# A convolution and two expert layers in one kernel: the last group of one product is put behind the next middle stage, and seven input steps run ahead

## The chip, the cores and the metric

One NeuronCore of a Trainium2 chip runs the whole kernel as one program. The metric is device time in microseconds (us): of several runs the median counts. A profiled execution gives the trace that is read here; its times are counted from the start of its span. The engines are named as the profile names them: PE is TensorE (PEld its weight loads), DVE VectorE, ACT ScalarE, POOL GpSimd, SP SyncE; a q behind a name is the engine's own queue (SPq issues loads, ACTq and POOLq issue the DMAs of their engines).

## The reference: what is computed

```
Xf = rfft(x, n=2S); Hf = rfft(h, n=2S)      # x: 4 batches, S=5696 positions, D=128 channels
y  = irfft(Xf * Hf)[:, :S, :]               # causal convolution along the sequence
x  = moe(y.reshape(22784, 128))             # 8 experts, each takes at most 2848 tokens, in order of logit
out = moe2(x)                               # 8 experts, one per token, times its softmax weight
```

The change concerns the convolution alone. Its transform of length S = 89 * 64 is done as matrix products: a product over 89 positions (matrix F), a middle stage over 64 (matrices E, a multiplication by the transform of h, and EI), and a product back (matrix G).

## The kernel before, in words

The four batches are worked in two pairs; pair 0 is batches 0 and 1, pair 1 batches 2 and 3. `A` is one buffer in SBUF of 128 partitions x 89 x 256, and both pairs use it. Each pair passes three stages.

- **First product, `s1`** (one call per batch, 256 columns of A are two calls). 16 steps per batch: a step is 16 matmuls with F (line 99) into one PSUM tile, whose two halves are copied into A by ACT and by DVE (line 103). Four steps share one load of the input, `XB<-in_xl` (line 94). A trace counts each of these f32 matmuls twice, so a step is 32 there.
- **Middle stage, `s2`.** 23 groups of four frequencies: matmuls with E on A (line 145), multiplication by the transform of h by DVE (line 148, with `hh` loaded by line 138), sums on POOL (lines 149 and 150), matmuls with EI (line 158), a copy back into A by ACT (lines 159 and 160), and a store `Z<-A` to DRAM on ACT's queue (line 161). Between the groups of the second middle stage a search for the routing thresholds is woven in (`head.step`): DVE's small instructions, an ACT pass over VT (line 417) and two PE matmuls (line 384).
- **Last product, `s3`.** 16 groups and a closing step. A group loads `XB<-Z` in two halves (line 172; every half reads rows of all frequencies, so it needs every `Z<-A` of its pair), does 32 matmuls with G (line 179; 64 in a trace), a DVE copy of 712 columns (line 183), and, one step later, the logits of the columns that are complete (lines 195, 197, 201, 203), their transposes into rows (line 220), a copy by ACT or DVE (lines 222, 223) and a store `yrow<-m` on POOL's queue (line 225). Columns left over from a group, `carry`, are copied to the front of the next (line 182).

Six buffers XB are shared in turn by the input loads, the E loads (line 135) and the Z loads. `ps` is a pool of four PSUM tiles that all stages share; a new tile waits until the tile four before it has been copied out. `m` is a pool of three SBUF buffers, shared by line 148 and by the rows of line 225.

The order is written out by `together` (line 226): it runs `ahead` steps of the first generator, then one step of the second and `r` of the first in turn. `together(nextpair(), s3(0), 2, 4)` joins the last product of pair 0 with the first product of pair 1: four steps ahead, then two per group. Then come the second middle stage `s2(1)` and `s3(1)`. Each engine and each queue runs its instructions in the order in which they stand; a scheduler at build time moves them a little by its own costs, which is why the order of the built program is shown below.

The part behind the convolution (the routing and the two expert layers) is the same in both kernels. Its gathers and scatters of single rows (lines 777, 759, 958) are DMAs whose descriptors POOL writes into a scratch area of SBUF.

Of the kernel before, what the change touches and what calls it, by code (L numbers as in the profile page):

```python
# [11 lines left out]
F32 = mybir.dt.float32  # L12
# [41 lines left out]
def first(b):  # L54

    return -(N1*b//N2)


def conv(tc,nc,a,yrow,LG,head):

    ctx=contextlib.ExitStack()
    with ctx:
        cp=ctx.enter_context(tc.tile_pool(name="cc",bufs=1))
        Hd=ctx.enter_context(tc.tile_pool(name="cd",bufs=1,space=bass.MemoryType.DRAM)).tile([128,23,2,2,128],F32,name="Hd")
        Z=[ctx.enter_context(tc.tile_pool(name=f"cz{i}",bufs=1,space=bass.MemoryType.DRAM)).tile([96,132,256],F32,name=f"Z{i}") for i in range(2)]
# [11 lines left out]
        def pads():  # L77

            zt=work("m"); nc.gpsimd.memset(zt,0.0)
            for i in range(2):  # L80
              for k in (89,93): nc.scalar.dma_start(Z[i][k:min(k+4,96),:128].rearrange("k r e -> r k e"),zt[:,:256*(min(k+4,96)-k)].rearrange("p (k e) -> p k e",e=256))
        XB=[cp.tile([128,2048],F32,name=f'XB{i}') for i in range(6)]
        nx=[0]
        def buf():
            nx[0]+=1; return XB[nx[0]%6]
        WS=dict(xs=1224,m=1040)
        def work(nm,w=1024): return wk.tile([128,WS.get(nm,1024)],F32,name=nm)[:,:w]
        def apart(i,mine,other):
            tc.declare_no_dep(i.ins,group=other,reason='other columns of A'); tc.add_to_no_dep_group(mine,i.ins)
        def s1(src,col,free=False):  # L90

            for g in range(4):
                xt=buf()[:96].rearrange("p (d n) -> p d n",n=64); cuts=(0,8,32) if col==128 and not g else (0,32)
                for d0,d1 in zip(cuts,cuts[1:]): nc.sync.dma_start(xt[:,d0:d1],src[:,g*2048+d0*64:g*2048+d1*64].rearrange("p (d n) -> p d n",n=64))
                for q in range(4):
                    p=ps.tile([128,2,512],F32,name="ps")
                    for i in range(8):
                        for c in range(2):
                            nc.tensor.matmul(p[c*64:c*64+64,i//4,(i%4)*89:(i%4)*89+89], xt[:,q*8+i,:], F[:,c*89:c*89+89], start=True,stop=True)  # L99
                    for u in range(2):  # L100
                        c0=col+g*32+q*8+4*u
                        o=A[:,:,c0:c0+4]; i=p[:,u,:356].rearrange("p (v k) -> p k v",v=4)
                        w=nc.scalar.activation(o,i,AF.Copy) if u==0 else nc.vector.tensor_copy(o,i)
                        if free: apart(w,'x0','h')
                    yield
# [22 lines left out]
        def s2(pr,step):  # L128
# [23 lines left out]
            def back(g):  # L152
                m=ST.pop(g); k,n,nq,P=part(g)
                pb=ps.tile([128,2,2,256],F32,name="ps")
                for q in range(nq):
                    for r in range(2):
                        for t in range(min(2,n-2*q)):
                            nc.tensor.matmul(pb[:,t,q],EI[t*64:t*64+64,r],m[t*64:t*64+64,q,2*r:2*r+2],start=r==0,stop=r==1)
                if n>1: nc.scalar.activation(A[:,k:k+n,:].rearrange("p (q t) e -> p q t e",t=2),pb.rearrange("p t q e -> p q t e"),AF.Copy)
                else: nc.scalar.activation(A[:,k:k+1,:],pb[:,0,0:1],AF.Copy)  # L160
                nc.scalar.dma_start(Z[pr][k:k+n,:128].rearrange("k r e -> r k e"),A[:,k:k+n,:])
            lag=3
            for i in range(ng+lag):
                step(i)
                if i<ng: forth(i)
                if i>=lag: back(i-lag)
        def s3(pr,step):

            st=dict(carry=0,prev=None,done=0)
            def spread(g):  # L170
                Bt=buf()[:96].rearrange("p (c j e) -> p c j e",j=4,c=2)
                for c in range(2): nc.sync.dma_start(Bt[:,c],Z[pr][:,c*64+4*g:c*64+4*g+4])
                py=ps.tile([128,8,128],F32,name="ps")
                for j in range(4):
                    w=first(4*g+j)+A0
                    for b in range(2):
                        for c in range(2):
                            for t in (0,64):
                                nc.tensor.matmul(py[t:t+64,j*2+b,:89],Bt[:,c,j,b*128+t:b*128+t+64],G[:,c,w:w+89],start=c==0,stop=c==1)  # L179
                carry=st['carry']; tot=carry+712  # L180
                yT=work("xs",1224)
                if carry: nc.vector.tensor_copy(yT[:,:carry],st['prev'])
                nc.vector.tensor_copy(yT[:,carry:carry+712].rearrange("p (a b) -> p a b",b=89),py[:,:,:89])
                new=[]
                for o in range(0,tot,512):
                    n=min(4,(tot-o)//128)
                    if n==4 or g==15 and n: new.append((yT[:,o:o+n*128],n,pr*89+st['done'])); st['done']+=n
                o=sum(n for _,n,_ in new)*128
                st.update(carry=tot-o,prev=yT[:,o:tot])
                return new  # L190
            def logits(sets):

                p=ps.tile([128,2,512],F32,name="ps"); lt=wk.tile([128,384],F32,name="lt",bufs=2)
                for s,(y,n,_) in enumerate(sets):
                    for j in range(n): nc.tensor.matmul(p[32*j:32*j+32,0,s*128:s*128+128],WG,y[:,j*128:j*128+128],start=True,stop=True)
                f=sum(n==4 for _,n,_ in sets)*128
                if f: nc.vector.tensor_copy(lt[:,:f],p[:,0,:f])
                if f<len(sets)*128: nc.vector.tensor_copy(lt[:32*n,f:f+128],p[:32*n,0,f:f+128])
                return p,lt,sets
            def columns(p,lt,sets):  # L200
                for s,(_,n,_) in enumerate(sets): nc.tensor.transpose(p[:,1,s*128:s*128+32*n],lt[:32*n,s*128:s*128+128],head.Ib[:32*n,:32*n])
                n=sum(n for _,n,_ in sets); col=sets[0][2]
                nc.vector.tensor_copy(LG[:,:,col:col+n],p[:,1,:32*n].rearrange("p (c w) -> p w c",w=32)[:,:8])
                head.columns(col+n)
            new=[]
            for g in range(17):
                old=new; t=logits(old) if old else None
                if g<16: new=spread(g)
                step(g)
                if t:  # L210
                    columns(*t)
                    for u in range(0,len(old),2): rows(old[u:u+2])
                yield
            assert st['carry']==0 and st['done']==89
        def rows(sets):

            nch=sum(n for _,n,_ in sets); col=sets[0][2]
            pt=ps.tile([128,2,512],F32,name="ps"); rb=work("m",8*W1).rearrange("p (i w) -> p i w",w=W1)
            for u,(y,n,_) in enumerate(sets):
                for i in range(n): nc.tensor.transpose(pt[:,u,i*128:i*128+128],y[:,i*128:i*128+128],head.Ib)  # L220
                o=rb[:,4*u:4*u+n,:128]; i=pt[:,u,:n*128].rearrange("p (i d) -> p i d",d=128)
                if u or len(sets)==1: nc.scalar.activation(o,i,AF.Copy)
                else: nc.vector.tensor_copy(o,i)
            nc.gpsimd.tensor_copy(rb.bitcast(I32)[:,:nch,128:],idt[:,col:col+nch,:])
            nc.gpsimd.dma_start(yrow[col*128:(col+nch)*128,:].rearrange("(i p) w -> p i w",p=128),rb[:,:nch])
        def together(ga,gb,r,ahead=0):

            for _ in range(ahead): next(ga,None)
            for _ in gb:
                for _ in range(r): next(ga,None)  # L230
            for _ in ga: pass
        for i,_ in enumerate(s1(a['hl'],128)):
            if i==3: later()
        together(s2h(128),s1(a['xl'][0],0,True),2)
        for _ in s1(a['xl'][1],128): pass
        s2(0,lambda i: pads() if i==4 else None)
        def nextpair():
            for b in range(2): yield from s1(a['xl'][2+b],b*128)
        together(nextpair(),s3(0,lambda g: None),2,4)
        head.gen=head.presearch()  # L240
        s2(1,lambda i: head.step(i) if i%2==0 else None)
        for _ in s3(1,head.step): pass
        if head.gen: drain(head.gen)
        head.bounds()
# [47 lines left out]
class Head:  # L292
# [11 lines left out]
    def columns(h,done):  # L304

        h.turn()
        while h.n<len(h.CH) and h.CH[h.n][1]<=done:
            h.chunk(h.n); h.n+=1
# [45 lines left out]
    def step(h,_):  # L354

        while h.gen:
            r=next(h.gen,None)
            if r is None: h.gen=None
            elif r>1: break
# [718 lines left out]
```

## Time and profile before

| what | us |
|---|---|
| median of 3 runs | 1846.17 (1842.44 to 1848.68) |
| the profiled execution | 1849.38 |
| its span | 1847.6 |
| PE busy in the span | 1691.3 (92%) |
| DVE, ACT, POOL busy | 1215.6, 928.4, 918.9 |
| mean granted clock of PE | 0.956 |

The span is what the trace covers; the profiled execution's own time is 1.8 us longer. The three runs lie 6.2 us apart, about 0.3%. Granted clock 1.00 is 2.4 GHz and 0.50 is 1.2 GHz, at which every matmul takes twice as long.

### The profile page before, as it was taken

To read this page: it belongs to the slowest core of one execution; us is meant where nothing else is said; L and a number is where in the kernel's file an instruction comes from. 1 tells how busy PE (TensorE), PEld (TensorE's weight loads), DVE (VectorE), ACT (ScalarE), POOL (GpSimd) and SP (SyncE) were. 2 spreads that over 40 slices of the span, in tenths; PEclk is the share of its full clock that TensorE was granted. 3 is DMA by queue.
4 is the path that set the end of the run, shared out by engine and by line. 5 is a ranking of instruction groups with operands and counts; after the bars stand their busy time and mean duration, and the time that the engine had idled before them with its cause. 6 is when DMAs were issued, how large, how long until landed. Compare 5 with 4: busy or idle time off the path is not lost.

```text
span 1847.6 us, 38007 instructions
## 1 busy us (share of the span) xinstructions
PE 1691.3 (92%) x14006; PEld 1414.2 (77%) x14006; DVE 1215.6 (66%) x3168; ACT 928.4 (50%) x1951; POOL 918.9 (50%) x1123
## 2 busy tenths in 40 slices
PE   7989799997928998989999999999999999999996
PEld 7866688566816776877877777888888888888996
DVE  2356245782576977878987855567866666667885
ACT  2322222231226556566675664555555555566784
POOL 0146111561225374758677578355444444455884
PEclk9999899996958999999999999999999999999998
DMA  9966988458623222313223021041322223244672
GB/s 238 332 227 215 249 215 251 149 173 239 182 81 57 66 47 75 83 41 97 69 60 98 26 68 44 23 136 56 122 86 91 92 92 94 79 133 127 203 213 66
DMA packets 107171, 230.72 MB, mean 125 GB/s; under 512 B 30985, under 2 KB 60496, under 8 KB 104064
## 3 DMA queue, kind: packets, MB, share of 16 engines
q1 hardware_dynamic: 57392, 148.89, 27.5%
q0 software_dynamic: 23376, 53.09, 10.3%
q10 hardware_dynamic: 26208, 26.24, 4.2%
q8 instruction: 112, 1.84, 0.4%
q14 instruction: 83, 0.68, 0.1%
HBM read 154.88 MB, written 74.04 MB: 124 GB/s over the span
## 4 chain that ended last, share of the span: by engine, by line
PE 56%; DVE 8%; DMA 2%; issue 2%; POOL 2%; ACT 1%; DVEq 0%; POOLq 0%; ACTq 0%; SPq 0%
PE ph L670 8%; PE py L684 8%; PE ph L671 8%; PE ph L672 8%; PE py L682 8%; PE py L683 8%; PE tr L661 2%; PE tr L722 2%; DVE hl L675 1%; PE rt L953 1%; DVE M L476 1%; DMA xg<-yrow,idx 1%; POOL BK L759 1%; DMA Vd<-V 1%; PE rt L594 1%
## 5 line engine op out<-in xcount | busy, mean ns | idle before, releaser
L675 DVE SCALAR_TENSOR_TENSOR hl<-ph,hh 128x480 fp32r<-128x480 f32 (+3 forms) x848 | 519.4, 617 | 246.0 <-ACT hh L674 241.4
L674 ACT ACTIVATE hh<-ph 128x480 fp32r<-128x480 f32 (+3 forms) x848 | 455.7, 543 | 368.8 <-PE ph L672 353.4
L684 PE MATMUL py<-hl,w2h 128*128 128x480 f32 (+3 forms) x848 | 317.7, 375 | 19.1 <-DVE hl L675 18.4
L670 PE MATMUL ph<-xh,w1h 128*128 128x480 f32 (+3 forms) x848 | 327.7, 386 | 0.2 <-ACT xh L663 0.2
L682 PE MATMUL py<-hh,w2h 128*128 128x480 f32 (+3 forms) x848 | 320.9, 378 | 1.3 <-ACT hh L674 1.3
L671 PE MATMUL ph<-xh,w1l 128*128 128x480 f32 (+3 forms) x848 | 313.6, 370 | 0.0
L672 PE MATMUL ph<-xl,w1h 128*128 128x480 f32 (+3 forms) x848 | 313.0, 370 | 0.0
L683 PE MATMUL py<-hh,w2l 128*128 128x480 f32 (+3 forms) x848 | 310.8, 367 | 0.0
L958 POOL DMA_INDIRECT out_dram<-OR,ids x190 | 193.9, 1020 | 165.5 <-DVE OR L956 115.0
L759 POOL DMA_INDIRECT BK<-RB,pi x192 | 188.1, 980 | 66.0 <-issue 53.7
L777 POOL DMA_INDIRECT xg<-yrow,idx x192 | 186.3, 970 | 67.4 <-issue 48.4
L684 PEld LDWEIGHTS py<-hl,w2h 128*128 128x128 f32 x848 | 161.3, 190 | 49.9 <-DVE hl L675 26.6
L672 PEld LDWEIGHTS ph<-xl,w1h 128*128 128x128 f32 x848 | 161.8, 191 | 22.2
L682 PEld LDWEIGHTS py<-hh,w2h 128*128 128x128 f32 x848 | 161.4, 190 | 21.5 <-ACT hh L674 1.8
L683 PEld LDWEIGHTS py<-hh,w2l 128*128 128x128 f32 x848 | 161.6, 191 | 19.2
L671 PEld LDWEIGHTS ph<-xh,w1l 128*128 128x128 f32 x848 | 162.5, 192 | 17.6
L635 POOL TENSOR_TENSOR w2l<-w2r,w2h 128x512 fp32r<-128x512 f32 x102 | 130.1, 1294 | 91.8 <-ACT w2h L634 91.7
L670 PEld LDWEIGHTS ph<-xh,w1h 128*128 128x128 f32 x848 | 162.1, 191 | 16.7 <-ACT xh L663 0.6
L99 PE MATMUL ps<-F,XB 96*64 96x89 f32 x2560 | 117.0, 250 | 20.7 <-issue 14.1
L99 PEld LDWEIGHTS ps<-F,XB 96*64 96x64 f32 x2560 | 110.1, 144 | 26.4 <-issue 23.1
L179 PE MATMUL ps<-G,XB 96*64 96x89 f32 x2048 | 98.0, 255 | 16.8 <-DMA XB<-Z 15.9
L179 PEld LDWEIGHTS ps<-G,XB 96*64 96x64 f32 x2048 | 90.4, 147 | 25.2 <-issue 22.7
(330 smaller groups left out, 2578.1 us busy)
## 6 DMA issues: line engine op xcount, KB each, us to landing
w1r<-in_moe_w_dram SPq DMA_DIRECT2D x51, 512.0 KB, 3.9
w2r<-in_moe_w2t_dram SPq DMA_DIRECT2D x51, 512.0 KB, 3.8
XB<-Z SPq DMA_DIRECT2D x64, 384.0 KB, 5.9
Z<-A ACTq DMA_DIRECT2D x44, 512.0 KB, 3.2
hh<-Hd SPq DMA_DIRECT2D x22, 512.0 KB, 3.8
XB<-in_xl_dram SPq DMA_DIRECT2D x14, 768.0 KB, 7.3
XB<-in_E_dram SPq DMA_DIRECT2D x10, 1024.0 KB, 6.5
xg<-BK SPq DMA_DIRECT2D x37, 260.0 KB, 2.7
```

The costliest lines, as they stand in the source:

```text
L99: nc.tensor.matmul(p[c*64:c*64+64,i//4,(i%4)*89:(i%4)*89+89], xt[:,q*8+i,:], F[:,c*89:c*89+89], start=True,stop=True)
L179: nc.tensor.matmul(py[t:t+64,j*2+b,:89],Bt[:,c,j,b*128+t:b*128+t+64],G[:,c,w:w+89],start=c==0,stop=c==1)
L670: nc.tensor.matmul(ph[:,:N],w1h[:,fs],xh[:,:N],start=True,stop=False)
L671: nc.tensor.matmul(ph[:,:N],w1l[:,fs],xh[:,:N],start=False,stop=False)
L672: nc.tensor.matmul(ph[:,:N],w1h[:,fs],xl[:,:N],start=False,stop=True)
L674: nc.scalar.activation(hh[:,:N],ph[:,:N],AF.Relu)
L675: LD[0]=nc.vector.scalar_tensor_tensor(hl[:,:N],ph[:,:N],0.0,hh.bitcast(F32)[:,:N],op0=ALU.max,op1=ALU.subtract)
L682: nc.tensor.matmul(py[:,:N],w2h[:,fs],hh[:,:N],start=f==0,stop=False)
L683: nc.tensor.matmul(py[:,:N],w2l[:,fs],hh[:,:N],start=False,stop=False)
L684: nc.tensor.matmul(py[:,:N],w2h[:,fs],hl[:,:N],start=False,stop=f==7)
L759: s=nc.gpsimd.indirect_dma_start(out=BK[:,:],out_offset=bass.IndirectOffsetOnAxis(ap=pi[:k,b:b+1],axis=0),in_=RB[:k,b,:W1],in_offset=None)
L958: sc=nc.gpsimd.indirect_dma_start(out=out[:,:],out_offset=bass.IndirectOffsetOnAxis(ap=ids[:,b:b+1],axis=0),in_=OR[:,b,:],in_offset=None,b ...
```

## The change

Four things are changed. The program reserves 4096 bytes of SBUF per partition for the descriptors of POOL's DMAs, where nothing was named before. `s3` can hold its last group back: with `hold=15` it closes the logits of the columns that group 14 has completed at once, copies the left-over 440 columns into a buffer of their own (`cy`, 2 KB per partition) and stops there; group 15 and the closing step run after `s2(1)`. The load of group 15's operand is issued inside `s2(1)`. Seven steps of the first product stand ahead of `s3(0)` in place of four, and the input load of the first is issued inside `s2(0)`.

```diff
+        def xload(src,g,cuts=(0,32)):
+            xt=buf()[:96].rearrange("p (d n) -> p d n",n=64)
+            for d0,d1 in zip(cuts,cuts[1:]): nc.sync.dma_start(xt[:,d0:d1],src[:,g*2048+d0*64:g*2048+d1*64].rearrange("p (d n) -> p d n",n=64))
+            return xt
...
+        BT={}
+        def operand(pr,g):
+            BT[pr,g]=buf()[:96].rearrange("p (c j e) -> p c j e",j=4,c=2)
+            for c in range(2): nc.sync.dma_start(BT[pr,g][:,c],Z[pr][:,c*64+4*g:c*64+4*g+4])
...
+                if hold and g==hold-1:
+                    finish(logits(new),new); new=[]
+                    cy=cp.tile([128,512],F32,name="cy")[:,:st['carry']]; nc.vector.tensor_copy(cy,st['prev']); st['prev']=cy
+                    yield 1
+                yield 0
...
-            for _ in gb:
+            for v in gb:
+                if v: break
...
-        s2(0,lambda i: pads() if i==4 else None)
+        XT={}
+        def hook0(i):
+            if i==4: pads()
+            if i==21: XT[0]=xload(a['xl'][2],0)
+        s2(0,hook0)
...
-        together(nextpair(),s3(0,lambda g: None),2,4)
+        pair0=s3(0,lambda g: None,15)
+        together(nextpair(),pair0,2,7)
         head.gen=head.presearch()
-        s2(1,lambda i: head.step(i) if i%2==0 else None)
+        def hook1(i):
+            if i==21: operand(0,15)
+            if i%2==0: head.step(i)
+        s2(1,hook1)
+        for _ in pair0: pass
...
-    nc = _bacc.Bacc("TRN2", target_bir_lowering=False, num_devices=1)
+    nc = _bacc.Bacc("TRN2", target_bir_lowering=False, num_devices=1, dynamic_dma_scratch_size=4096)
```

The line numbers of the changed kernel are higher: its lines 102, 187, 203, 209, 233, 148 and 161 are the lines 99, 179, 195, 201, 220, 145 and 158 of before; 344, 460, 463 and 407 are 321, 437, 440 and 384; 92, 141 and 174 are 94, 138 and 172.

**First place: PE from the end of s2(0) into s3(0).** XB_107 to XB_111 are the shared buffers; `F` marks the first product, `G` the last. Before:

```order
L158 MATMUL ps<-m,EI 128x256 x26
L99 MATMUL ps<-F,XB_107 64x89 x64
L179 MATMUL ps<-G,XB_108 64x89 x2
L99 MATMUL ps<-F,XB_109 64x89 x15
L179 MATMUL ps<-G,XB_108 64x89 x30
L99 MATMUL ps<-F,XB_109 64x89 x17
L195 MATMUL ps<-xs,WG 32x128 x4
```

Now:

```order
L161 MATMUL ps<-m,EI 128x256 x26
L102 MATMUL ps<-F,XB_107 64x89 x64
L102 MATMUL ps<-F,XB_108 64x89 x48
L187 MATMUL ps<-G,XB_109 64x89 x32
L102 MATMUL ps<-F,XB_108 64x89 x16
L102 MATMUL ps<-F,XB_110 64x89 x16
L203 MATMUL ps<-xs,WG 32x128 x4
```

Three more steps (48 matmuls) stand ahead of the first matmul with G.

**The same place, SP's queue.** Before, the third input load (into XB_106) stands behind the `hh` loads of s2(0) and in front of the last two that were fetched for s2(1):

```order
L138 DMA hh<-Hd 128x1024 x4
L94 DMA XB_109<-in_xl_dram 96x2048
L138 DMA hh<-Hd 128x1024 x3
L138 DMA hh<-Hd 64x2x128
L138 DMA hh<-Hd 128x1024
L94 DMA XB_106<-in_xl_dram 96x2048
L138 DMA hh<-Hd 128x1024 x2
L172 DMA XB_108<-Z_88 96x1024 x2
```

Now it goes into XB_110, whose last reader in s2(0) is group 15 and not the last group, and stands earlier:

```order
L141 DMA hh<-Hd 128x1024 x4
L92 DMA XB_110<-in_xl_dram 96x2048
L141 DMA hh<-Hd 128x1024
L141 DMA hh<-Hd 64x2x128
L141 DMA hh<-Hd 128x1024 x3
L174 DMA XB_109<-Z_88 96x1024 x2
```

The third input load has moved in front of the last five `hh` loads, two of s2(0) and three of s2(1); the Z loads still come last.

**Second place: PE at the end of s3(0) and the start of s2(1).** Before, from group 15's matmuls with G on:

```order
L179 MATMUL ps<-G,XB_106 64x89 x32
L201 MATMUL ps<-Ib,lt 128x128
L220 MATMUL ps<-Ib,xs 128x128 x4
L195 MATMUL ps<-xs,WG 32x128 x9
L321 MATMUL ps<-Ib,Vc 128x128
L220 MATMUL ps<-Ib,xs 128x128 x2
L201 MATMUL ps<-Ib,lt 128x128 x2
L201 MATMUL ps<-Ib,lt 128x32
L220 MATMUL ps<-Ib,xs 128x128 x3
L437 MATMUL ps<-Ib,mmh 2x128
L220 MATMUL ps<-Ib,xs 128x128 x4
L440 MATMUL ps<-Ib,m2b 128x2
```

Now, from the end of group 14's matmuls with G on:

```order
L187 MATMUL ps<-G,XB_111 64x89 x23
L209 MATMUL ps<-Ib,lt 128x128
L233 MATMUL ps<-Ib,xs 128x128 x4
L203 MATMUL ps<-xs,WG 32x128 x4
L233 MATMUL ps<-Ib,xs 128x128 x4
L209 MATMUL ps<-Ib,lt 128x128
L344 MATMUL ps<-Ib,Vc 128x128
L460 MATMUL ps<-Ib,mmh 2x128
L463 MATMUL ps<-Ib,m2b 128x2
L148 MATMUL ps<-A,XB_106 64x256 x16
```

Both pieces are followed by the first matmuls of s2(1). Group 15 and the 9 logit blocks of its columns are gone from here.

**Third place: PE behind s2(1).** Before, the first matmuls of s3(1) (two of them, then the search's two) followed the last with EI directly. Now:

```order
L161 MATMUL ps<-m,EI 128x256 x10
L187 MATMUL ps<-G,XB_106 64x89 x32
L203 MATMUL ps<-xs,WG 32x128 x3
L233 MATMUL ps<-Ib,xs 128x128 x3
L203 MATMUL ps<-xs,WG 32x128 x6
L233 MATMUL ps<-Ib,xs 128x128 x2
L209 MATMUL ps<-Ib,lt 128x128 x2
L209 MATMUL ps<-Ib,lt 128x32
L233 MATMUL ps<-Ib,xs 128x128 x4
L187 MATMUL ps<-G,XB_107 64x89 x2
L407 MATMUL ps<-sg,blkr 128x2
```

Group 15 of pair 0 stands between the middle stage and the first operand of pair 1 (XB_107). From there on the order of every engine is that of before.

## Rows read from the trace of the kernel before

**Rows 1.** The page: PE's busy time, and the closing chain by engine.

```profile
PE 1691.3 (92%) x14006; PEld 1414.2 (77%) x14006; DVE 1215.6 (66%) x3168; ACT 928.4 (50%) x1951; POOL 918.9 (50%) x1123
...
PE 56%; DVE 8%; DMA 2%; issue 2%; POOL 2%; ACT 1%; DVEq 0%; POOLq 0%; ACTq 0%; SPq 0%
```

**Rows 2.** Windows: length, busy PE, PEld, DVE, ACT, POOL; clock, DMA, GB/s.

```profile
200.40:207.40 7.00, 0.03 (x2) 0.00 (x0) 1.84 (x4) 1.54 (x4) 0.00 (x0) 0.65 0.67 193
207.40:212.80 5.40, 5.36 (x73) 5.39 (x73) 0.00 (x0) 0.00 (x0) 0.00 (x0) 0.50 1.04 250
...
331.50:336.00 4.50, 0.09 (x3) 0.05 (x1) 4.36 (x8) 1.02 (x3) 3.12 (x3) 0.96 0.18 72
336.00:342.50 6.50, 6.50 (x30) 4.16 (x32) 1.71 (x6) 1.73 (x3) 2.50 (x2) 0.50 0.53 164
...
419.10:427.60 8.50, 0.00 (x0) 0.00 (x0) 0.00 (x0) 1.13 (x2) 0.00 (x0) 0.61 0.66 201
427.60:451.70 24.10, 22.46 (x260) 19.64 (x262) 6.91 (x29) 2.12 (x4) 1.74 (x3) 0.50 1.04 260
```

**Rows 3.** Timeline, s2(0) into s3(0): start, length, engine, line, operation [idle before].

```profile
188.80 0.34 SPq L94 DMA_DIRECT2D XB<-in_xl_dram  x1
...
195.30 5.13 PE L99 MATMUL ps<-F,XB 96*64 96x89 f32 x128
...
203.66 1.54 ACT L103 ACTIVATE A<-ps 128x356 f32<-128x356 f32 x4 [7.80 <-DMA Z<-A]
204.16 1.84 DVE L103 COPY A<-ps 128x356 f32<-128x356 f32 x4 [12.08 <-ACT A L103]
...
207.44 0.57 PE L179 MATMUL ps<-G,XB 96*64 96x89 f32 x4 [7.01 <-DMA XB<-Z]
...
215.10 0.42 PE L195 MATMUL ps<-xs,WG 128*32 128x128 f32 x8
...
218.76 2.67 PE L99 MATMUL ps<-F,XB 96*64 96x89 f32 x64
```

**Rows 4.** Windows as in Rows 2: the first boundary, and s3(0).

```profile
188.00:202.00 14.00, 12.33 (x184) 10.41 (x182) 3.50 (x4) 4.17 (x5) 5.27 (x7) 1.00 0.89 289
206.00:300.00 94.00, 88.31 (x1855) 79.55 (x1857) 37.62 (x93) 18.13 (x37) 11.42 (x23) 0.96 0.90 228
```

**Rows 5.** Timeline, the end of s3(0) and the start of s2(1).

```profile
312.13 0.90 DVE L183 COPY xs<-ps 128x712 f32<-128x712 f32 x1 [1.86 <-PE ps L179]
313.06 0.39 DVE L182 COPY xs<-xs 128x440 f32<-128x440 f32 x1
...
316.16 0.90 DVE L183 COPY xs<-ps 128x712 f32<-128x712 f32 x1 [2.31 <-PE ps L179]
...
319.17 0.30 PE L321 MATMUL ps<-Ib,Vc 128*128 128x128 f32 x1 [1.43 <-DVE Vc L315]
...
322.03 3.67 PE L145 MATMUL ps<-A,XB 128*64 128x256 f32 x32
...
324.73 1.23 DVE L148 TENSOR_TENSOR m<-ps,hh 128x1024 f32<-128x1024 f32 x1 [1.73 <-DMA yrow<-m]
```

**Rows 6.** Timeline, the end of s2(1) and the start of s3(1).

```profile
416.22 2.85 PE L158 MATMUL ps<-m,EI 64*128 64x256 f32 x20
...
423.76 24.70 SPq L172 DMA_DIRECT2D XB<-Z  x18
...
427.66 0.57 PE L179 MATMUL ps<-G,XB 96*64 96x89 f32 x4 [8.59 <-DMA XB<-Z]
...
429.01 4.72 PE L179 MATMUL ps<-G,XB 96*64 96x89 f32 x60 [0.27 <-DMA XB<-Z]
```

**Rows 7.** Instructions on yrow: duration ns min/median/max; then who waited: us, times.

```profile
L777 POOL DMA_INDIRECT xg<-yrow,idx x192: 922/947/1727, 552.8 to 1217.7; - x192
L225 POOL DMA_DIRECT2D yrow<-m x34: 553/763/901, 220.0 to 513.0; - x34
...
  PE tr L661: 11.0, 10
```

More of the change, by code (lines that the diff above doesn't have):

```diff
@@ L89, in apart, with s1 @@
             tc.declare_no_dep(i.ins,group=other,reason='other columns of A'); tc.add_to_no_dep_group(mine,i.ins)
-        def s1(src,col,free=False):
+        def xload(src,g,cuts=(0,32)):
+            xt=buf()[:96].rearrange("p (d n) -> p d n",n=64)
+            for d0,d1 in zip(cuts,cuts[1:]): nc.sync.dma_start(xt[:,d0:d1],src[:,g*2048+d0*64:g*2048+d1*64].rearrange("p (d n) -> p d n",n=64))
+            return xt
+        def s1(src,col,free=False,ready={}):
             for g in range(4):
-                xt=buf()[:96].rearrange("p (d n) -> p d n",n=64); cuts=(0,8,32) if col==128 and not g else (0,32)
-                for d0,d1 in zip(cuts,cuts[1:]): nc.sync.dma_start(xt[:,d0:d1],src[:,g*2048+d0*64:g*2048+d1*64].rearrange("p (d n) -> p d n",n=64))
+                xt=ready[g] if g in ready else xload(src,g,(0,8,32) if col==128 and not g else (0,32))
                 for q in range(4):
@@ L166, in s2, with s3 @@
                 if i>=lag: back(i-lag)
-        def s3(pr,step):
+        BT={}
+        def operand(pr,g):
+            BT[pr,g]=buf()[:96].rearrange("p (c j e) -> p c j e",j=4,c=2)
+            for c in range(2): nc.sync.dma_start(BT[pr,g][:,c],Z[pr][:,c*64+4*g:c*64+4*g+4])
+        def s3(pr,step,hold=None):
             st=dict(carry=0,prev=None,done=0)
             def spread(g):
-                Bt=buf()[:96].rearrange("p (c j e) -> p c j e",j=4,c=2)
-                for c in range(2): nc.sync.dma_start(Bt[:,c],Z[pr][:,c*64+4*g:c*64+4*g+4])
+                if (pr,g) not in BT: operand(pr,g)
+                Bt=BT[pr,g]
                 py=ps.tile([128,8,128],F32,name="ps")
@@ L204, in columns, with finish @@
                 head.columns(col+n)
+            def finish(t,old):
+                columns(*t)
+                for u in range(0,len(old),2): rows(old[u:u+2])
             new=[]
@@ L209, in s3 @@
                 step(g)
[L210 to L213, printed above, removed]
+                if t: finish(t,old)
+                if hold and g==hold-1:
[3 more added lines that the diff above has]
+                yield 0
             assert st['carry']==0 and st['done']==89
@@ L235, in conv @@
         for _ in s1(a['xl'][1],128): pass
-        s2(0,lambda i: pads() if i==4 else None)
+        XT={}
[3 more added lines that the diff above has]
+        s2(0,hook0)
         def nextpair():
-            for b in range(2): yield from s1(a['xl'][2+b],b*128)
-        together(nextpair(),s3(0,lambda g: None),2,4)
+            for b in range(2): yield from s1(a['xl'][2+b],b*128,ready={} if b else XT)
+        pair0=s3(0,lambda g: None,15)
+        together(nextpair(),pair0,2,7)
         head.gen=head.presearch()
-        s2(1,lambda i: head.step(i) if i%2==0 else None)
+        def hook1(i):
[3 more added lines that the diff above has]
+        for _ in pair0: pass
         for _ in s3(1,head.step): pass
```

## The prediction

> **What bounds the kernel now.** I read the page first: TensorE is busy for 92% of the span, and the chain that ended last runs mostly over it [rows 1]. So time is won only where PE stands still or runs slowly, and the change touches three such places in the convolution. For these I read the windows (busy time beside the granted clock), then the timeline around each. The windows show PE standing still for 7.0 us at the first boundary and 8.5 us at the second, and after each a stretch at half clock (1.2 GHz): 5.4 us and 24.1 us [rows 2]. The timeline names the cause of both stops: PE waits for the first Z load of a last product (7.01 and 8.59 us), and that load waits for the last store of the middle stage before it [rows 3, 6]. Between them lies the start of s2(1), where PE waits 1.43 us for DVE, and where group 15 of pair 0 stands in front of the first matmul with E [rows 5].
>
> **First place: seven steps ahead.** Nothing is added; three steps change place. Before, four steps fill the four PSUM tiles in 5.13 us, 1.28 each, and PE then stops at 200.43, because the copies into A wait for the stores of A (ACT starts at 203.66) [rows 3]. So the three new steps cannot start in the first half of the gap. They start when one tile has been copied: four ACT copies take 1.54 us and DVE starts 0.50 after ACT, four in 1.84, so about 1.0 us after the stores have landed. Before, at 215.10, PE has done six steps and group 0; three steps more (two take 2.67, so 4.0) make that 219.1 for nine steps and group 0.
> - Worst: the stores land as before, and PE works from 204.6 at half clock for the 5.4 us that it took before [rows 2]. That is two steps; the third ends at 211.4. Group 0 (2.7 us, half of rows 6's 4.72 and 0.57) ends at 214.1, two more steps at 216.8. Gain 2.3 us.
> - Best: the third input load leaves the critical stretch. Before it is issued at 188.80, as soon as the last E matmul has read its buffer, and its 786 KB share the DMA engines with the last stores, at 289 GB/s [rows 3, 4]: 2.7 us. Now it waits for group 15, seven groups earlier. With the stores landed at 200.9 the steps run from 201.9 to 205.8 at full clock. Group 0 needs both halves of its operand, which came 5.3 us after the stores (the first 3.9 after; the second 1.35 later, as 427.66 and 429.01 at the other boundary [rows 6]), so it ends at 208.9, the two steps at 211.6. Gain 7.5.
>
> I take 4.3, nearer to the worst, since a stop of about 2 to 4 us remains and with it probably a stretch at half clock. On SP the moved load passes `hh` loads; it waits for a matmul that is done long before their buffers come free, so I cost that at nothing; if it did block, the last multiplications would be late by its wait.
>
> **Second place: group 15 leaves the start of s2(1).** Removed from here: 32 matmuls with G, a DVE copy, nine logit blocks, nine transposes. But the search's first steps still depend, through DVE and PE in turn, on the columns of the last group worked, and the matmuls with E stand behind them. Before, that chain runs from DVE's copy of group 15 at 316.16 to the first matmul with E at 322.03, 5.87 us. Now it starts at the copy of group 14, at 312.13 [rows 5]: 318.0, so 4.0 earlier. Added on DVE is the copy to `cy`, 0.39 like the copy of the same 440 columns that goes; it now stands in the chain, and some copies of group 15 no longer do. I take 3.7. Besides, DVE's first multiplication waited 1.73 us for a row store that still held its buffer; with fewer rows that may go: best 5.7. Worst: PE has little to do for some 3 us of the new chain, and falls to half clock. The first 32 matmuls then take 3.67 more [rows 5], and nothing is left: 0. An idle stretch of 4.5 us did end in 6.5 us at half clock in this stage [rows 2], so that is not remote; but DVE, with four multiplications of 1.23, paces this start too, so much of it would lie beside DVE.
>
> **Third place: group 15 behind s2(1).** The added 2.7 us of matmuls and some 2.5 us of logits and transposes start when the last matmul with EI ends, at 419.07, and must be done by 427.66, when the first Z load has landed [rows 6]. They fit with about 3 us to spare, with DVE idle in that window [rows 2]: cost nothing. If their operand were late it would be 2.7 us at most; it is loaded early in s2(1), once group 3 has read the buffer. What queues behind them is s3(1), which waits for the DMA anyway. The row stores of 9 blocks (600 KB) now meet the Z loads, at 260 GB/s 2.3 us: cost 0 to 2.3, I take 0.5. The open price is the clock. PE at half clock is busy 22.46 us; at full clock up to 11.2 go. But 18 loads in 24.7 us use the DMA engines at 1.04 [rows 2, 6], so I bound the real gain by 8. I take 1.5 of it: the last 3 us before the first Z load stay idle, and so probably the clock still falls. Net gain 1.0.
>
> The Trainium skill, "TensorE: Matmul & The Clock Gate", section "What's actually happening", says that throttled is the default state and activity releases it. Here PE was busy 22.46 of 24.10 us and stayed at half clock, so I do not lean on that rule; by it the stretch would shrink, and the time would be that of rival B.
>
> **The scratch.** A smaller descriptor area saves no time by itself. Gathers take 0.95 us in the middle, 1.73 at most; row stores 0.76 and 0.90 [rows 7]: no sign of waiting for room before. Bounds: 0 (no wait with the small area either) to rival D. I take 0.
>
> **Sum.** 4.3 + 3.7 + 1.0 = 9.0 us. The profiled execution took 1849.4, so its like would take 1840.4. It lies 3.2 above the median of 1846.2; the gains do not depend on that, so the forecast is 1846.2 - 9.0 = 1837.2. The bounds add up to 7.5 + 5.7 + 8 = 21.2 on one side and 2.3 + 0 - 2.3 = 0 on the other.
>
> **Rivals.**
> - B: with group 15 in the gap the clock holds (or comes back quickly) and s3(1) starts at full speed: the 1.0 of the third place becomes 8, time 1830. For it: the gap's longest idle piece falls from 8.5 to about 3 us. Against: 4.5 us of idleness were enough for half clock, 3 may be.
> - C: the gains are absorbed. In s3(0) the DMA engines work at 0.90 over 94 us [rows 4]; if they and not PE pace it, work moved ahead only waits later. With half clock at the start of s2(1) on top, about 3 us are left: 1843. Against: PE is busy for 88.31 of those 94 us.
> - D, slower: POOL waits for room in the small area before it writes descriptors. It decides once more DMAs are in flight than the area holds, so first where four gathers of a tile follow each other. If every gather then took the longest seen, 1.73 in place of 0.95, a tile's four would come 3.1 us later. PE already waits for gathered rows 10 times, 11.0 us in all [rows 7]; ten waits 3.1 us longer are 31 us: 1846 - 9 + 31 = 1868. "Perfetto Trace Analysis" of the Trainium skill, section "DMA Instruction — SWDGE (GPSIMD)", speaks for it: more descriptors can be generated than the buffer holds. "DMA: Bandwidth & Descriptors" (SWDGE path) gives 16 bytes per descriptor; my estimate from that is 256 per engine in 4096 bytes, against 65 for a store of eight row blocks, of which three buffers allow three at a time. No run here shows the limit; by the estimate there is room.
>
> **Chances.** Forecast 0.52, B 0.16, C 0.23, D 0.09. About 0.3%, 5.5 us, is what a measurement of this kernel can tell from no change. The forecast lies beyond that with most of its spread (0.44 of 0.52), B wholly, C hardly (0.03): faster 0.63, slower 0.09 (D), the rest 0.28. The range goes from 1827, past B, to 1848, past C and the spread of the runs; D stays outside.
>
> **What would show it.** At the first boundary three steps with F before the first matmul with G, starting about 1 us after ACT's copies begin, and an earlier start of these copies. The first matmul with E about 8 us earlier in the span than 322.0. Group 15 between the last matmul with EI and the first Z load's landing, and a gap of about 3 us behind it. The clock row of the start of s3(1) decides between the forecast and B. L777, L759 and L958 at their old durations would clear D. I am wrong if s2(1) starts less than 4 us earlier, or if what it gains is lost again before 505.

## The result, and the profile after

The changed kernel takes 1829.0 us (median of 4 runs, 1825.7 to 1831.3), the kernel before 1845.0 on the same chip (4 runs, 1842.4 to 1848.7): ratio 0.9901, 95% interval 0.9880 to 0.9922. The medians are 16.0 us apart; the ratio stands for 18 us (14 to 22). Forecast were 9.0. So the time lies inside the range, and the gain is about twice the forecast.

The two profiled executions are 19.2 us apart: spans of 1847.6 and 1828.4 us. The lines of the changed kernel are shifted: L99 is now L102, L103 is L106, L145 is L148, L158 is L161, L179 is L187, L195 is L203, L321 is L344, L958 is L981. To find the 19.2 us, I took the start of the same instruction in both traces at each stage's end:

| instruction | before | after | lead |
|---|---|---|---|
| last four matmuls with E of s2(0) | 187.69 | 185.88 | 1.8 |
| first matmul with E of s2(1) | 322.03 | 311.03 | 11.0 |
| last matmuls with EI of s2(1) | 416.22 | 404.98 | 11.2 |
| last whole group of 64 matmuls with G | 505.52 | 494.31 | 11.2 |
| first expert matmul (`ph`) | 564.41 | 554.62 | 9.8 |
| last scatter to `out` | 1832.34 | 1821.65 | 10.7 |
| end of the span | 1847.6 | 1828.4 | 19.2 |

The first 1.8 us arise at 130 us, ahead of anything that was moved: 16 matmuls with EI took 3.68 us before and 2.00 after. So the convolution's three places bring 9.4 us in this pair. And 8.5 us come where no term of the sum looked: behind the last scatter.

The page after, PE's busy time and the closing chain, to be held against [rows 1]:

```profile
PE 1686.4 (92%) x14006; PEld 1407.3 (77%) x14006; DVE 1212.3 (66%) x3169; ACT 928.0 (51%) x1951; POOL 919.9 (50%) x1123
...
PE 54%; DVE 8%; DMA 3%; POOL 2%; issue 2%; ACT 2%; DVEq 0%; SPq 0%; POOLq 0%; ACTq 0%
```

The same matmuls, 4.9 us less of busy time: PE worked a little less at half clock. That is a quarter of the 19.2, so most of the gain is standing time.

The first boundary after (timeline: start, length, engine, line, operation, count, and in brackets the idle time and what ended it), against [rows 3]:

```profile
185.88 1.08 PE L148 MATMUL ps<-A,XB 128*64 128x256 f32 x4
...
193.48 5.13 PE L102 MATMUL ps<-F,XB 96*64 96x89 f32 x128
201.58 5.55 PE L102 MATMUL ps<-F,XB 96*64 96x89 f32 x96 [2.97 <-DVE A L106]
206.96 2.63 PE L187 MATMUL ps<-G,XB 96*64 96x89 f32 x64
209.42 2.62 PE L102 MATMUL ps<-F,XB 96*64 96x89 f32 x64
211.97 0.42 PE L203 MATMUL ps<-xs,WG 128*32 128x128 f32 x8
...
200.49 1.54 ACT L106 ACTIVATE A<-ps 128x356 f32<-128x356 f32 x4 [6.46 <-DMA Z<-A]
```

Three steps stand in front of group 0, 1.1 us behind ACT's first copy. PE's longest stop is 2.97 us, not 7.01. From the start of the four steps to nine steps and group 0 it is 18.5 us; before, six steps and group 0 took 19.8, and three more 4.0: 5.3 us gained. ACT's copies wait 6.46 us for the stores of A, not 7.80: of the 2.7 us that the bound from above gave to an earlier store, 1.3 came.

The start of s2(1) after, on PE, against [rows 5]:

```profile
309.49 0.45 PE L344 MATMUL ps<-Ib,Vc 128*128 128x128 f32 x1 [2.06 <-DVE mmh L459]
310.86 0.23 PE L463 MATMUL ps<-Ib,m2b 2*128 2x2 f32 x1 [0.71 <-DVE m2b L462]
311.03 6.08 PE L148 MATMUL ps<-A,XB 128*64 128x256 f32 x32
```

The stage starts 11.0 us earlier (less 1.8 and 5.3, that leaves 3.9), and the first 32 matmuls with E take 6.08 us in place of 3.67, after a pause of 2.06: part of them ran at half clock. The window from 304 to 316 shows a granted clock of 0.72 (columns as in the windows below):

```profile
304.00:316.00 12.00, 9.23 (x77) 5.83 (x75) 6.10 (x21) 2.12 (x4) 2.61 (x4) 0.72 0.71 203
```

The stage loses nothing by it here: the lead is 11.2 at its end too. That DVE, whose multiplications pace the stage, hides it is argued and not shown.

The end of s2(1) and the start of s3(1) after, against [rows 6]; below it the windows (length, busy PE, PEld, DVE, ACT, POOL; granted clock, DMA share, GB/s), against the last ones of [rows 2]:

```profile
404.98 2.85 PE L161 MATMUL ps<-m,EI 64*128 64x256 f32 x20
407.76 2.68 PE L187 MATMUL ps<-G,XB 96*64 96x89 f32 x64
...
416.93 0.37 PE L187 MATMUL ps<-G,XB 96*64 96x89 f32 x4 [2.89 <-DMA XB<-Z]
418.27 4.17 PE L187 MATMUL ps<-G,XB 96*64 96x89 f32 x60 [0.65 <-DMA XB<-Z]
...
449.96 4.42 PE L187 MATMUL ps<-G,XB 96*64 96x89 f32 x54 [3.19 <-issue]
```

```profile
405.00:414.00 9.00, 8.48 (x115) 6.46 (x114) 4.22 (x15) 3.40 (x6) 2.69 (x7) 1.00 0.59 194
414.00:417.00 3.00, 0.11 (x3) 0.10 (x4) 0.00 (x0) 0.60 (x1) 0.90 (x1) 1.00 0.93 254
417.00:422.00 5.00, 4.35 (x60) 4.16 (x62) 0.65 (x4) 0.92 (x2) 0.19 (x1) 0.66 1.03 297
422.00:446.00 24.00, 22.37 (x429) 18.39 (x425) 11.56 (x39) 2.99 (x5) 4.02 (x7) 1.00 1.04 273
446.00:457.00 11.00, 7.81 (x98) 6.83 (x97) 2.95 (x9) 0.00 (x1) 1.15 (x3) 0.69 1.03 280
```

Group 15 fills the gap as forecast, 2.89 us stay idle, and PE gets its first Z load 9.1 us after the last matmul with EI has ended (8.6 before). What follows is rival B's picture: the clock is low for a few us and then full, where it stayed at 0.50 for 24.1 us before. Yet nothing is won. At 450 PE stands for 3.19 us with nothing to wait for but its own instructions ("issue"), falls to half clock again, and by 494 the lead is the 11.2 us that it was at 405.

The end of both kernels (timeline of POOL, the last row of each), the kernel before first:

```profile
1832.34 0.97 POOL L958 DMA_INDIRECT out_dram<-OR,ids  x1 [0.31 <-issue]
```

```profile
1821.65 0.97 POOL L981 DMA_INDIRECT out_dram<-OR,ids  x1 [0.30 <-issue]
```

The last scatter ends at 1833.3 and 1822.6; the spans end 14.3 and 5.8 us later. In windows from there to the end, before first:

```profile
1833.30:1835.30 2.00, 0.00 (x0) 0.00 (x0) 0.00 (x0) 0.00 (x0) 0.01 (x1) 0.70 0.06 15
1835.30:1837.30 2.00, 0.00 (x0) 0.00 (x0) 0.00 (x0) 0.00 (x0) 0.00 (x0) 0.50 0.04 12
1837.30:1847.60 10.30, 0.00 (x0) 0.00 (x0) 0.00 (x0) 0.00 (x0) 0.00 (x0) 0.50 0.00 0
```

```profile
1822.60:1824.60 2.00, 0.00 (x0) 0.00 (x0) 0.00 (x0) 0.00 (x0) 0.02 (x1) 0.50 0.07 15
1824.60:1826.60 2.00, 0.00 (x0) 0.00 (x0) 0.00 (x0) 0.00 (x0) 0.00 (x0) 0.50 0.05 12
1826.60:1828.40 1.80, 0.00 (x0) 0.00 (x0) 0.00 (x0) 0.00 (x0) 0.00 (x0) 0.50 0.00 0
```

The scattered rows take the same 4 us to land. Then no engine is busy and no DMA moves anything: for 10.3 us in the kernel before, for 1.8 in the changed one. These windows leave out what the engines' queues do. The last lines of the program, asked by line, show two long instructions in POOL's queue: a semaphore step (`INC_SWDGE_SEM`) and, among three drains, one that is long (count, duration in ns as min/median/max, first and last start in us). The kernel before first:

```profile
L854 POOLq INC_SWDGE_SEM  x1: 2395/2395/2395, 1835.3 to 1835.3; - x1
L1074 POOLq DRAIN  x3: 46/107/9057, 1837.7 to 1847.3; - x3
```

```profile
L877 POOLq INC_SWDGE_SEM  x1: 720/720/720, 1824.7 to 1824.7; - x1
L1097 POOLq DRAIN  x3: 46/107/2197, 1825.4 to 1828.2; - x3
```

They stand one behind the other and take 11.45 us before and 2.92 after: the 8.5 us.

### The profile page after: what moved, and what is told of

It reads as the page before. It is cut to its first block, busy times and chain, and to the rows that moved or that the text cites. A ratio compares the mean times of both kernels' runs of the same rounds, so it can differ in the third digit from the quotient of the medians.

```text
span 1828.4 us, 38014 instructions
## 1 busy us (share of the span) xinstructions
PE 1686.4 (92%) x14006; PEld 1407.3 (77%) x14006; DVE 1212.3 (66%) x3169; ACT 928.0 (51%) x1951; POOL 919.9 (50%) x1123
## 4 chain that ended last, share of the span: by engine, by line
PE 54%; DVE 8%; DMA 3%; POOL 2%; issue 2%; ACT 2%; DVEq 0%; SPq 0%; POOLq 0%; ACTq 0%
PE ph L693 8%; PE py L707 8%; PE ph L694 8%; PE ph L695 8%; PE py L705 8%; PE py L706 8%; PE tr L684 2%; PE tr L745 2%; DVE hl L698 2%; POOL BK L782 1%; PE rt L976 1%; DMA xg<-yrow,idx 1%; DVE M L499 1%; DMA VT<-Vd 1%; DMA Vd<-V 1%
## 5 line engine op out<-in xcount | busy, mean ns | idle before, releaser
L981 POOL DMA_INDIRECT out_dram<-OR,ids x190 | 194.0, 1021 | 166.4 <-DVE OR L979 115.2
L694 PEld LDWEIGHTS ph<-xh,w1l 128*128 128x128 f32 x848 | 162.4, 191 | 17.5
L102 PE MATMUL ps<-F,XB 96*64 96x89 f32 x2560 | 115.9, 250 | 22.0 <-issue 11.6
L102 PEld LDWEIGHTS ps<-F,XB 96*64 96x64 f32 x2560 | 109.2, 144 | 27.9 <-issue 20.4
L152 POOL TENSOR_TENSOR m<-m,xs 128x512 f32<-128x512 f32 (+1 forms) x46 | 57.4, 1249 | 96.0 <-DVE xs L151 84.4
L440 ACT ACTIVATE jk<-VT,th 128x1424 bf16<-128x1424 f32 (+3 forms) x52 | 67.8, 1303 | 72.3 <-DVE th L436 37.2
```

The costliest lines, as they stand in the source:

```text
L694: nc.tensor.matmul(ph[:,:N],w1l[:,fs],xh[:,:N],start=False,stop=False)
L981: sc=nc.gpsimd.indirect_dma_start(out=out[:,:],out_offset=bass.IndirectOffsetOnAxis(ap=ids[:,b:b+1],axis=0),in_=OR[:,b,:],in_offset=None,b ...
```

## The experiments

Theory S: the descriptor area is paid for behind the last scatter, and the convolution brought about what was forecast. Rival T: the end is a trait of that execution or of the moved work, and the moved work made the whole gain. The runs came in three batches, on three chips, each with the kernel before beside it. There the kernel before takes 2055.9, 2057.7 and 2056.6 us. From the first gather to the first scatter to `out` the traces of these batches need 916 to 932 us, those of the first pair 722; the cause of that is open. Totals there scatter by 10 us and more, so stages are read from the traces. All stages of the 14 traces stand in a table behind the runs.

**The scratch alone**, 4096 and then 2048 bytes in the kernel before:

```diff
-    nc = _bacc.Bacc("TRN2", target_bir_lowering=False, num_devices=1)
+    nc = _bacc.Bacc("TRN2", target_bir_lowering=False, num_devices=1, dynamic_dma_scratch_size=4096)
```

> The kernel before with the scratch argument of 4096 bytes and nothing else. Theory S (the descriptor area itself costs time behind the last scatter: in the traces 14.3 us lie between the end of the last scatter and the end of the span before, 5.8 us after): this stretch is 5.8 us here too, all else as before, so about 8.5 us less than the kernel before, some 1836 us. Rival T (the stretch at the end belongs to the single run or to the moved work): it stays at 14 us and the time at 1845. Rival D (POOL waits for room in the small area): gathers and scatters lengthen and the time rises.

Measured: 2047.1 us, ratio 0.9966 (0.9948 to 0.9984), so 7.0 us less by the ratio (3.3 to 10.7). The last row of POOL, in a span of 2041.1, and below it the two rows of POOL's queue:

```profile
2034.09 0.97 POOL L958 DMA_INDIRECT out_dram<-OR,ids  x1 [0.30 <-issue]
```

```profile
L854 POOLq INC_SWDGE_SEM  x1: 720/720/720, 2037.3 to 2037.3; - x1
L1074 POOLq DRAIN  x3: 46/107/2197, 2038.0 to 2040.8; - x3
```

6.0 us lie behind the last scatter, and the two instructions last as long as in the changed kernel. Theory S holds as to the area, and T falls: nothing was moved here. Rival D of the prediction does not show: L777's median is 947 ns as before [rows 7], L958's 973 in both.

> The kernel before with 2048 bytes of scratch alone. Theory S with a cost in proportion to the size: if 4096 bytes give 5.8 us behind the last scatter, and the area that the kernel before has is four times as large, the slope is 8.5 us per 12288 bytes (0.69 us per KB), so 4.4 us here and a time about 9.9 us below the kernel before, some 1835. If the cost were a step and not a slope, 5.8 us as with 4096. Rival D: with half the room the gathers of a tile wait, POOL's L777, L759 and L958 rise above 1.0 us on the mean, and the time rises above that of 4096.

Measured: 2043.8, ratio 0.9953 (0.9929 to 0.9977); 4.4 us behind the last scatter, as the slope had it. The medians of L777 and L958 are 949 and 976 ns: no sign of waiting for room, even with half the area.

**The moved work with 14336 bytes**, in the changed kernel (4096 replaced in the line above):

> The changed kernel with 14336 bytes of scratch in place of 4096: the moved work almost without the smaller area. Theory S: 12.9 us behind the last scatter, the convolution as in the changed kernel; time 1829 + 7.1 = 1836, so the moved work gives some 9 to 10 us of the 16 to 18 by itself. Rival T: 1829, all of the gain is the moved work's.

Measured: 2037.5, ratio 0.9916 (0.9892 to 0.9940); 7.2 us behind the last scatter, in a span of 2039.9:

```profile
2031.71 0.97 POOL L981 DMA_INDIRECT out_dram<-OR,ids  x1 [0.30 <-issue]
```

Not the 12.9 of a slope, and not T's 5.8: a proportion to the size is refuted above 4096 bytes. Most of the fall lies between 14336 bytes and what the kernel before has.

**The changed kernel with 2048 bytes:**

> The changed kernel with 2048 bytes of scratch. Theory S: 4.4 us behind the last scatter, time about 1.4 below the changed kernel, some 1827.5. Rival D: gathers longer, time above 1829.

Measured: 2041.9, ratio 0.9947 (0.9927 to 0.9966); 4.7 us behind the last scatter. That is 1.2 us less there than with 4096, which the total is too coarse to show. Nor do the totals show the moved work here: the kernel before with the same 2048 bytes had 0.9953 in this batch. With 14336 bytes they do, 0.9916 against the 0.9966 of 4096 bytes alone. So these totals do not settle what the moved work is worth.

**The kernel before once more:**

> The kernel before, unchanged, profiled once more on the chip of these runs. If the stretch behind the last scatter belongs to the descriptor area, it is 14 us here as in the first trace; if it was a trait of that one execution, it is near the 6 to 7 us that 14336 and 4096 bytes gave. Its stages give the base for the others: 133.5 us from the last E matmul of s2(0) to the first of s2(1), 96.9 for s2(1), 89.3 from there to the last matmul with G.

Measured: 2064.6 in one run, span 2062.8. The last row of POOL, and the window behind what still lands:

```profile
2047.22 0.97 POOL L958 DMA_INDIRECT out_dram<-OR,ids  x1 [0.30 <-issue]
```

```profile
2052.20:2062.80 10.60, 0.00 (x0) 0.00 (x0) 0.00 (x0) 0.00 (x0) 0.00 (x0) 0.50 0.00 0
```

14.6 us again, 10.6 of them with no engine and no DMA at work, and the drain takes 9057 ns as in the first trace. So the long end belongs to the kernel without the argument.

**Only the steps ahead**: the changed kernel without group 15 held back, and without the scratch argument:

```diff
-        pair0=s3(0,lambda g: None,15)
+        pair0=s3(0,lambda g: None)
...
-            if i==21: operand(0,15)
...
-        for _ in pair0: pass
```

> Only the seven steps ahead and the earlier third load; group 15 stays in front of s2(1), and the scratch is that of the kernel before. The prediction's first term: the stretch from the last E matmul of s2(0) to the first of s2(1) is 4.3 us shorter than in the kernel before (the changed kernel's trace suggests 5), the rest as before, so 0.2 to 0.3% faster. Rival C (absorbed): the first boundary gains, the last step with F ends when it did, and no time is won.

Measured: 2061.3, ratio 1.000 (0.9974 to 1.0026); 14.5 us behind the last scatter. The first stretch is 128.0 us, 4.0 less than the mean of the kernel before's order, but only 1.1 less than in the kernel before on this chip (129.1); s2(1) takes 97.7. The total shows none of the 0.2 to 0.3% that were expected.

**Only group 15 held back** (`together(nextpair(),pair0,2,4)` and no load in `hook0`), with 8192 bytes:

> Only group 15 held back until s2(1) has ended, four steps ahead and the third load as before, with 8192 bytes of scratch. Prediction's second and third term: s2(1) starts 3.7 us earlier, and group 15 costs nothing behind it (from the last matmul with EI to the last with G 89 us as before, or less if the clock comes back sooner). Behind the last scatter: 6 to 8.6 us, against 14 in the kernel before, if the area decides. Together 10 to 12 us, 0.5 to 0.6% on a chip that takes 2050; without the area 4 us, 0.2%.

Measured: 2047.2, ratio 0.9951 (0.9921 to 0.9982). 7.3 us behind the last scatter, the same as with 14336. The first stretch is 2.7 us shorter than the mean of before, s2(1) 2.4 longer, and s3(1) takes 88.7.

**The changed kernel again:**

> The changed kernel, unchanged, on the same chip as the others of this call: 1.0% below the kernel before if the gain is the same on every chip; 5.8 us behind the last scatter. If the middle of the program (routing and the first experts' gathers) takes what the convolution gains on this chip, 0.5%.

Measured: 2048.3, ratio 0.9932 (0.9905 to 0.9959), and 5.8 us at the end. With the third batch's 0.9933 below, the gain is 14 us on these chips by the ratios and 18 in the first pair; the intervals overlap.

**Steps ahead with 4096 bytes, and the same without the load in `hook0`:**

```diff
-            if i==21: XT[0]=xload(a['xl'][2],0)
```

> The seven steps ahead, the earlier third load and the 4096 bytes, without group 15 held back: the changed kernel less one part. If holding group 15 back wins what the prediction says (3.7 + 1.0), this is 4.7 us (0.23%) above the changed kernel of the same call, with s2(1) starting 3 to 4 us later against the end of s2(0). If what the earlier start of s2(1) wins is given back inside s2(1) (the stages of the other runs: 98 us after an early start, 95 to 97 after a late one), the two are equal. Behind the last scatter 5.8 us.

> As the one before, but the third input load of the next pair is issued where it was. If the load in the critical stretch cost the prediction's 1.5 to 2.7 us, the stores of A land and ACT's first copy starts that much later after the last E matmul than with the earlier load (14 to 15 us there), and the first matmul with G comes later; if not, both are equal and the three steps alone make the gain of the first place.

Measured: 2042.9, ratio 0.9930 (0.9910 to 0.9950), and 2048.6 in one run. The first is level with the changed kernel of its batch (0.9933), so holding group 15 back shows no gain in the total, though the changed order starts s2(1) some 4.6 us sooner. The second failed as an experiment: all five engines' orders come out the same in both programs, the hook alone moves nothing. It is of use as a measure: two traces of one order, 132.2 and 129.2 us in the first stretch, 317.6 and 312.2 up to the last matmul with G. That is how far one trace can be trusted.

**Dummy matmuls behind group 14**, in the changed kernel:

```diff
+                    pw=ps.tile([128,8,128],F32,name="ps")
+                    for j in range(2):
+                        w=first(4*g+j)+A0
+                        for b in range(2):
+                            for c in range(2):
+                                for t in (0,64): nc.tensor.matmul(pw[t:t+64,j*2+b,:89],BT[pr,g][:,c,j,b*128+t:b*128+t+64],G[:,c,w:w+89],start=c==0,stop=c==1)
```

> The changed kernel with 16 more matmuls with G (1.4 us at full clock), whose result nothing reads, right behind group 14, where PE otherwise waits about 2 us for the search. If the half clock at the start of s2(1) comes from this pause and costs time, the first 32 matmuls with E take 3.7 us in place of 5 to 6 and s2(1) is up to 2 us shorter; if DVE's four multiplications pace the start, s2(1) lasts the same; if the dummies stand in the way of the search's steps, it starts up to 1.4 us later.

Measured: 2038.1, ratio 0.9919 (0.9901 to 0.9937). The timeline of its PE at the start of s2(1):

```profile
303.99 1.29 PE L230 MATMUL ps<-G,XB 96*64 96x89 f32 x28
306.11 0.30 PE L350 MATMUL ps<-Ib,Vc 128*128 128x128 f32 x1 [0.82 <-DVE mmh L465]
...
307.45 3.67 PE L148 MATMUL ps<-A,XB 128*64 128x256 f32 x32
```

The pause shrinks from 2.06 to 0.82 us, the clock holds, and the 32 matmuls take 3.67 us. s2(1) is 96.0 us long against 97.4 on the mean: 1.4 less, as the first theory of the expectation had it, though one trace is no proof.

> The changed kernel as it is, for the comparison inside this call: 0.7 to 1.0% below the kernel before; 5.8 us behind the last scatter; 124 to 125 us from the last E matmul of s2(0) to the first of s2(1), 97 to 98 for s2(1), 87 to 89 from there to the last matmul with G.

Measured: 2041.9, ratio 0.9933 (0.9913 to 0.9953), 6.0 us at the end. The dummies are 3.8 us below it by the medians, but the intervals overlap, and 4.3 us of lead in their trace arise ahead of the first matmul with E of s2(0). That the dummies make a faster kernel is not shown.

**The stages of the 14 traces**, worked out from the starts of the first and last such matmul: I from the last matmul with E of s2(0) to the first of s2(1), II to the last with EI, III to the last with G. Means, and the range in brackets; us.

| order | traces | I | II | III | I to III |
|---|---|---|---|---|---|
| before (two scratch runs with it) | 4 | 132.0 (129.1–134.7) | 95.5 (94.7–96.7) | 88.5 (87.6–89.3) | 316.0 |
| ahead only | 3 | 129.8 (128.0–132.2) | 96.7 (95.4–97.7) | 87.5 (86.3–88.4) | 313.9 |
| hold only | 1 | 129.2 | 97.9 | 88.7 | 315.8 |
| changed | 5 | 125.2 (124.1–128.1) | 97.4 (96.4–99.5) | 89.1 (87.3–89.9) | 311.7 |
| changed, with dummies | 1 | 124.5 | 96.0 | 85.9 | 306.4 |

**The end of the 14 traces**, in us: the two instructions of POOL's queue, which last the same in every trace of one size, and the whole stretch behind the last scatter.

| bytes named | traces | semaphore step | long drain | behind the last scatter |
|---|---|---|---|---|
| none | 3 | 2.40 | 9.06 | 14.3, 14.6 and 14.5 |
| 14336 | 1 | 0.92 | 3.01 | 7.2 |
| 8192 | 1 | 1.02 | 3.42 | 7.3 |
| 4096 | 7 | 0.72 | 2.20 | 5.8 to 6.0 |
| 2048 | 2 | 0.42 | 0.97 | 4.4 and 4.7 |

## Why the prediction was right or wrong

- **The scratch: the step that failed.** "A smaller descriptor area saves no time by itself", "I take 0", with a bound of 0 on the side of a gain. It is worth 8.5 us in the first pair (14.3 to 5.8), and as much between the means of three and seven traces (14.4 and 5.9). I looked only for a loss, on the engines' rows, and took no row from the stretch behind the last scatter, which the trace of before shows: 11.45 us of it are a semaphore step and a drain in POOL's queue, and they take 2.92 with 4096 bytes. With 8.5 the forecast would have been 1846.2 - 17.5 = 1828.7; 1829.0 was measured.
- **First place: 4.3 forecast, 5.3 in the first pair**, inside its bounds. The mechanism was right: three steps about 1 us behind ACT's copies, at half clock for part of the time. The stores landed 1.3 us earlier, half of the best case. The part of it that I gave to the moved load is not told from the steps, since the hook alone changes no order.
- **Second place: 3.7 forecast, 3.9.** The chain from DVE's copy of group 14 (305.33 now) to the first matmul with E takes 5.70 us, where 5.87 was read from group 15. I and II together, however: stage I is 6.8 us shorter over all traces (8.0 forecast), and stage II 1.9 longer. That give-back was in my bound (half clock at the start) but not in my value. The dummies, in one trace, bear on 1.4 of the 1.9; the rest is open.
- **Third place: 1.0 forecast, 0.0 in the first pair, -0.6 over all traces.** The work fits the gap as said. In the first pair the clock went as rival B had it, and the 8 us did not come. The moved work does not decide the clock: of the five traces of the changed order two stay at half clock for 10 us longer than the other three, and the kernel before shows both cases too. In windows (columns as above) of the scratch-only run with 4096 bytes, and then of the kernel before again:

```profile
431.00:439.00 8.00, 7.69 (x159) 6.60 (x159) 3.54 (x18) 0.60 (x1) 0.99 (x2) 1.00 1.04 243
447.00:457.00 10.00, 7.16 (x127) 5.58 (x127) 4.03 (x11) 1.20 (x2) 1.85 (x3) 0.98 1.05 274
```

```profile
428.00:436.00 8.00, 7.89 (x87) 6.55 (x87) 1.97 (x8) 0.52 (x1) 0.00 (x0) 0.50 1.04 268
445.00:455.00 10.00, 9.91 (x179) 8.12 (x177) 4.52 (x11) 1.20 (x2) 2.05 (x4) 1.00 0.80 242
```

  One order of work, and about 15 us into the stage once at full clock and once at half; stage III took 89.3 and 87.6 us. The run that went fast early is idle later, while the DMA engines are still at 1.05, and then stands for its instructions:

```profile
457.76 4.16 PE L179 MATMUL ps<-G,XB 96*64 96x89 f32 x53 [2.93 <-issue]
```

  The 14 traces say the same. Between 20 and 30 us after the last matmul with EI seven of them show a granted clock of 1.00, seven 0.50 to 0.56; stage III takes 87.9 us on the mean of the first seven and 88.8 of the others. So some 10 us of full clock in place of half are worth about 1 us here. The reading that fits is a stretch bound by its DMAs, whose engines stand at 1.04 early in the stage at either clock and take back what the clock gives; it is argued, since no run changed the load. That instructions come late because they share these engines was not tried either.
- **Rival C** comes nearest in size, not in mechanism. It left about 3 us, lost in s3(0) and at the start of s2(1). Over all traces 4.3 us of the convolution's 9.0 are left (the means of 4 and 5 traces, each spread over 6 to 7 us, so the size is not settled): 1.2 are missing in stage I, and stages II and III give back 1.9 and 0.6. In the first pair it was 9.4. So part of the agreement in that pair is luck, and two profiles alone would not have told.
- **Rival D** is out: gathers at a median of 947 ns, PE waiting 11.6 us (11 times) for gathered rows, against 11.0 (10). With 2048 bytes the medians of gathers and scatters are 949 and 976.

## What to carry to other kernels

Read the stretch between the last busy instruction and the end of the span as a stage of its own, the engines' queues with it, and when a change touches something that is set up or taken down once per program, look there and at the start for its price. Ask of a clock stretch what else is full in it: where the DMA engines stood at 1.04 here, PE's clock was worth about 1 us of a stage of 88. And take a gain of a few us from several traces: two traces of one order were 5 us apart here.

## What the runs showed of the hardware

- With 2048, 4096, 8192 and 14336 bytes of descriptor area the program ends 4.5, 5.9, 7.3 and 7.2 us behind its last scatter (means), and 14.4 without the argument. All but 2.8 to 3.3 us of it is one semaphore step and one drain in POOL's queue (11.45 us without the argument, 2.92 with 4096 bytes). What the drain does in that time, and why it is shorter with 14336 bytes than with 8192, stays open. The Trainium skill, "SBUF — State Buffer", section "SBUF size: 192, 224, or 256?", reckons 16 KiB for this area; no run here shows how large that of the kernel before is. The Trainium skill also says, in "Runtime: NRT & Kernel Launch", section "The ~15µs preamble/postamble breakdown", that DMA rings are reset behind a kernel, at about 2 us; no row here is named so, and whether the drain is part of it is not shown.
- With 2048 bytes gathers (949 ns) and scatters (976 ns) are as fast, by their medians, as with the area of the kernel before (947 and 973).
- The same program takes 1845 us in the first pair's runs and 2056 on the chips of the later ones, with the difference between the first gather and the first scatter to `out` (722 us in the first pair's traces, 916 to 932 in the later ones).
